# Loads through one ring, uneven groups and moved casts in an attention and feed-forward kernel

## The chip, the cores and the metric

The kernel runs on one core of a Trainium2 chip. A core has a matrix engine (PE, whose weight loads are shown as PEld), a vector engine (DVE), a scalar engine (ACT), a general-purpose engine (POOL) and a queue that issues transfers (SP); each works through its own instructions in order and waits on semaphores for the others. Sixteen DMA engines move data between HBM and the on-chip memory. The metric is device microseconds of one execution; lower is better.

## The reference

Inputs are q, k, v of shape (4, 8, 768, 64) in float32 and three weight matrices. Each head attends causally; the retrieval heads (0, 2 and 6) see all earlier keys, the five streaming heads only the first 4 keys and a window of 64. The result, as 3072 tokens of 512, goes through a gated feed-forward block.

```python
scores = scale * np.matmul(q, k.transpose(0, 1, 3, 2))
in_win = (rel >= 0) & (rel < int(window))          # window 64
stream_keep = causal & (is_sink | in_win)          # 4 sinks
mask = np.where(retrieval_head, causal, stream_keep)
a = softmax(np.where(mask, scores, -1e9))
x = np.matmul(a, v)      # to (B*S, H*D) = (3072, 512)
g = x @ w_gate           # (512, 1536)
out = (g * sigmoid(g) * (x @ w_val)) @ w_out       # (1536, 512)
```

## The kernel before, in words

**Units.** The 3072 tokens are 24 tiles of 128 (TT = 24; six per batch, i is the index in the batch). A tile goes through these steps; each is one item of a list:

- `load` (L74): three transfers of 256 KB on SP bring the tile's q, k and v in float32 into a ring of four landing buffers. Tiles 0 to 3 are loaded at the start; `cast(t)` issues the load of tile t + 4.
- `cast` (L186): q and k are cast to float16 on DVE (hq, L192, 512 elements each), v on POOL (vt, L196).
- `transposes` (L201): eight PE transposes of q and k, and a copy to qkT on DVE (L210); POOL then copies the sink keys and values (k2, v2: L213, L216 for i = 0) or the second half of the tile (L221, L223) into operands that hold "sinks and the tail of the previous tile" for streaming heads.
- `scores` (L256), one to four units a tile: up to eight 128x128 score blocks on PE into the one scores buffer in PSUM, exp on ACT (L272, L276) into e; masks are deferred to the next flush. In the first unit of a tile all blocks are masked at once on POOL (L281 for i = 0, L287 otherwise); in later units, one head's pair on POOL (L296) and the diagonal block of each retrieval head on DVE (L299), three a tile for i > 0.
- `values` (L306), for the odd and the even heads: matmuls of e with v, then reciprocal and a scaled copy on DVE (xb, L317, L318).
- `xtranspose` (L324): four transposes and a DVE copy to xt (L332), the feed-forward's input.

**The order of items.** For tile t the list interleaves its scores units with values of t-1 (even), transposes of t+1, values of t (odd) and xtranspose of t-1. cast(t+2) stands just before the transposes of t+1, so a cast is a whole tile ahead of its use.

**Groups.** The feed-forward takes four tiles at a time (GT = 4, six groups). The *lead* is all attention items through xtranspose(3), run alone, with a flush after each item; by the order above it also holds tile 4's scores and tile 5's transposes. Then for each group g and each of 12 blocks j: `gate` (four matmuls of 512 columns, tanh on ACT, L410), a *beat*, `val` (four matmuls, then sil L421 and h L424 on DVE), a beat, `outproj` of group g-1 (four matmuls, L436; every third one ends an output tile, which ACT copies, L441, and SP stores), a beat. Each beat flushes masks and runs a share of the attention items for the tiles of group g + 1. Three PSUM buffers serve gate and val, one the output, one the scores, one all transposes. After the last group its 48 output matmuls run alone.

**Weights.** They come as 18 pieces of 512 KB through their own ring of five landing buffers (`wload`, L143), and are cast to float16: gate pieces on DVE (L161), val and out pieces on POOL (L165, L158). `wstep` casts the next piece and loads up to five ahead; it is called with 4 after the lead and with 2 after each j of group 0:

```python
    lead = ends[GT - 1]
    for n in range(lead):
        attend(n + 1)
        flush()
    wstep(4)
```

**Constants.** POOL builds the identity, the masks (diag, band0, m1, and m0 by eight copies, L121) and fills k2 and v2 with zeros (L131, L132) before its first cast.

Of the kernel before, what the change touches and what calls it, by code (L numbers as in the profile page):

```python
# [7 lines left out]
FP = mybir.dt.float32  # L8
# [7 lines left out]
def kernel(  # L16
# [27 lines left out]
    GT = 4  # L44
    NG = TT // GT
# [9 lines left out]
    wstage = ctx.enter_context(tc.tile_pool(name="wstage", bufs=5))  # L55
    raw = ctx.enter_context(tc.tile_pool(name="raw", bufs=4))
# [15 lines left out]
    raws = {}  # L72

    def load(t):  # L74
        b, i = divmod(t, NT)
        sl = slice(i * 128, (i + 1) * 128)
        qk = raw.tile([128, 2, 8, 64], FP, name="rawqk", tag="rawqk")
        vr = raw.tile([128, 8, 64], FP, name="rawv", tag="rawv")
        nc.sync.dma_start(out=qk[:, 0], in_=q[b, :, sl, :].rearrange("h s d -> s h d"))
        nc.sync.dma_start(out=qk[:, 1], in_=k[b, :, sl, :].rearrange("h s d -> s h d"))  # L80
        nc.sync.dma_start(out=vr, in_=v[b, :, sl, :].rearrange("h s d -> s h d"))
        raws[t] = (qk, vr)

    for t in range(4):
        load(t)
# [34 lines left out]
    for n_, src in enumerate((band0, band0, band0, diag, band0, band0, diag, diag)):  # L120
        nc.gpsimd.tensor_copy(out=m0[:, n_, :], in_=src)  # L121
# [7 lines left out]
    for n in range(2):  # L129
        nc.gpsimd.memset(vt[n][:, :, :, 64:66], 1.0)  # L130
        nc.gpsimd.memset(k2[n], 0.0)  # L131
        nc.gpsimd.memset(v2[n], 0.0)  # L132


    wg_sb = const.tile([128, 4, DFF], FH, name="wg_sb")
    wv_sb = const.tile([128, 4, DFF], FH, name="wv_sb")
    wo_sb = const.tile([128, NJ, DM], FH, name="wo_sb")
    wgd = moe_w_gate.rearrange("(po p) n -> p po n", p=128)
    wvd = moe_w_val.rearrange("(po p) n -> p po n", p=128)
    wod = moe_w_out.rearrange("(po p) n -> p po n", p=128)  # L140
    staged = {}

    def wload(kind, c):  # L143
        st = wstage.tile([128, 1024], FP, name="wst", tag="wst")
        if kind == "o":
            nc.sync.dma_start(
                out=st.rearrange("p (a n) -> p a n", a=2), in_=wod[:, 2 * c:2 * c + 2, :])
        else:
            d = wgd if kind == "g" else wvd
            nc.sync.dma_start(  # L150
                out=st.rearrange("p (a n) -> p a n", a=4),
                in_=d[:, :, c * 256:(c + 1) * 256])
        staged[kind, c] = st

    def wcast(kind, c):
        st = staged.pop((kind, c))
        if kind == "o":
            nc.gpsimd.tensor_copy(  # L158
                out=wo_sb[:, 2 * c:2 * c + 2, :], in_=st.rearrange("p (a n) -> p a n", a=2))
        elif kind == "g":  # L160
            nc.vector.tensor_copy(  # L161
                out=wg_sb[:, :, c * 256:(c + 1) * 256],
                in_=st.rearrange("p (a n) -> p a n", a=4))
        else:
            nc.gpsimd.tensor_copy(  # L165
                out=wv_sb[:, :, c * 256:(c + 1) * 256],
                in_=st.rearrange("p (a n) -> p a n", a=4))

    worder = [(kd, c) for c in range(NJ // 2) for kd in "gv"] + [("o", c) for c in range(NJ // 2)]
    wnext = [0, 0]  # L170

    def wstep(n=1):

        for _ in range(n):
            if wnext[1] >= len(worder):
                return
            while wnext[0] < len(worder) and wnext[0] < wnext[1] + 5:
                wload(*worder[wnext[0]])
                wnext[0] += 1
            wcast(*worder[wnext[1]])  # L180
            wnext[1] += 1
# [4 lines left out]
    def cast(t):  # L186

        b, i = divmod(t, NT)
        qk, vr = raws.pop(t)
        hq = half.tile([128, 2, 2, 256], FH, name="hq", tag="hq")  # L190
        for n in range(2):
            nc.vector.tensor_copy(  # L192
                out=hq[:, n].rearrange("p r (k d) -> p r k d", d=64),
                in_=qk[:, n].rearrange("p (k r) d -> p r k d", r=2),
            )
        nc.gpsimd.tensor_copy(out=vt[b % 2][:, i, :, 0:64], in_=vr)  # L196
        halves[t] = hq
        if t + 4 < TT:
            load(t + 4)
# [56 lines left out]
    def scores(t, u, unit):  # L256
# [22 lines left out]
        def masks():  # L279
            if i == 0:  # L280
                nc.gpsimd.tensor_tensor(  # L281
# [3 lines left out]
            if u == 0:  # L285
                ev = e.rearrange("p s (h n) q -> p (s h) (n q)", n=2)
                nc.gpsimd.tensor_tensor(  # L287
# [4 lines left out]
            for s in range(2):  # L292
                for n, (h, m, total, _, _) in enumerate(unit[s]):
# [4 lines left out]
                    elif m == total - 1:  # L298
                        nc.vector.tensor_tensor(  # L299
# [24 lines left out]
    def xtranspose(t):  # L324
        g, n = divmod(t, GT)
        if g not in xts:
            xts[g] = xtp.tile([128, 4, GT * 128], FH, name="xt", tag="xt")
# [9 lines left out]
    def add(cost, f, *a):  # L337
        items.append((cost, f, a))

    def tile_items(t):  # L340
        ss = []
        if t < TT:
            units = plan_of(t)
            ss = [(0.3, scores, (t, u, None)) for u in range(len(units))]
        other = []
        if t > 0:
            other.append((0.4, values, (t - 1, 0)))
        if t + 1 < TT:
            other.append((0.5, transposes, (t + 1,)))
# [163 lines left out]
```

## Time and profile before

| | us |
|---|---|
| median of 3 runs (lowest to highest) | 317.99 (317.45 to 320.77) |
| the profiled execution | 320.0 |
| its span, first to last instruction | 318.3 |
| PE busy | 263.1 (83%) |
| DVE busy | 212.0 (67%) |
| ACT busy | 116.3 (37%) |
| POOL busy | 132.5 (42%) |

A row of a view in order of time gives start, length, engine, line, operation, output, inputs, count, and in brackets the idle time ahead of it and what ended it. A row of the groups gives busy time and the mean in ns, and then the idle time before the group's instructions. A row of the chain gives start, length and what was on the path that set the end. A PE row's length contains about 0.24 us of pipeline beyond the streaming of its columns, so a run of matmuls is priced by the distance of their starts.

### The profile page before, as it was taken

What the parts mean: (1) busy time and instruction counts of PE and PEld (TensorE: products, weight loads), DVE (VectorE), ACT (ScalarE), POOL (GpSimd) and SP (SyncE); (2) the same over time, 40 slices, a digit from 0 to 9 for tenths busy, and PEclk for the clock granted to TensorE, in tenths of its full rate; (3) what the DMA queues carried; (4) which work ended last, traced back from release to release, by engine and by line L of the source; (5) the groups of instructions that cost most, each with busy time, mean ns of one, the idle gap of its engine ahead of it and who ended that gap; (6) DMA issues with size and microseconds to landing.
All of it is one profiled execution on the core that took longest, in us unless ns stands there. A gap on an engine that the chain in (4) does not pass through costs nothing.

```text
span 318.3 us, 5386 instructions
## 1 busy us (share of the span) xinstructions
PE 263.1 (83%) x2096; PEld 133.0 (42%) x2096; DVE 212.0 (67%) x402; ACT 116.3 (37%) x177; POOL 132.5 (42%) x152
## 2 busy tenths in 40 slices
PE   0035761976886999998999999999899998999984
PEld 0024541433442454453545444544445444444431
DVE  4996583699997666786878757777776655555500
ACT  1023441350431445534353445245344453333211
POOL 8885761585991540643535416445143030000000
PEclk9999999997998999999999999999999999999999
DMA  8996548999844045505552534000000000000021
GB/s 184 217 209 148 134 100 216 381 298 348 244 103 99 13 121 134 129 6 132 132 123 62 132 85 103 33 33 35 33 2 33 35 33 16 20 33 35 38 94 66
DMA packets 86328, 34.94 MB, mean 110 GB/s; under 512 B 75552, under 2 KB 81696, under 8 KB 86304
## 3 DMA queue, kind: packets, MB, share of 16 engines
q1 hardware_dynamic: 86304, 34.61, 40.0%
q8 instruction: 16, 0.26, 0.3%
q14 instruction: 8, 0.07, 0.1%
HBM read 28.31 MB, written 6.29 MB: 109 GB/s over the span
## 4 chain that ended last, share of the span: by engine, by line
PE 67%; DVE 14%; DMA 6%; POOL 5%; ACT 4%; SPq 1%; issue 1%; DVEq 0%; ACTq 0%; POOLq 0%
PE o_ps L436 20%; PE gate L406 18%; PE val L417 17%; DVE hq L192 8%; PE sc L266 6%; ACT e L272 3%; PE av L314 3%; PE tr L207 2%; DMA wst<-in_moe_w_val_dram 2%; DMA wst<-in_moe_w_out_dram 2%; DMA wst<-in_moe_w_gate_dram 2%; DVE h L424 2%; PE xtr L331 1%; DVE qkT L210 1%; DVE e L299 1%
## 5 line engine op out<-in xcount | busy, mean ns | idle before, releaser
L406 PE MATMUL gate<-xt,wg_sb 128*128 128x512 f16 x288 | 75.5, 385 | 12.6 <-DVE wg_sb L161 7.0
L421 DVE SCALAR_TENSOR_TENSOR sil<-sig,gate 128x512 f32<-128x512 f32 x72 | 49.2, 684 | 45.7 <-ACT sig L410 45.6
L410 ACT ACTIVATE sig<-gate 128x512 f32<-128x512 f32 x72 | 43.0, 597 | 100.2 <-PE gate L406 100.2
L417 PE MATMUL val<-xt,wv_sb 128*128 128x512 f16 x288 | 76.5, 389 | 1.8 <-DVE sil L421 1.8
L436 PE MATMUL o_ps<-wo_sb,h 128*128 128x512 f16 x288 | 73.4, 382 | 2.8 <-ACT o_sb L441 2.8
L287 POOL TENSOR_TENSOR e<-e,m 128x1024 f16<-128x1024 f16 x20 | 42.6, 2132 | 66.3 <-ACT e L272 66.3
L272 ACT ACTIVATE e<-sc 128x1024 f16<-128x1024 f32 x48 | 49.1, 1022 | 53.3 <-PE sc L266 49.1
L424 DVE SCALAR_TENSOR_TENSOR h<-sil,val 128x512 f16<-128x512 f32 x72 | 49.5, 688 | 8.4 <-PE val L417 0.7
L192 DVE CAST hq<-rawqk 128x512 f16<-128x512 f32 x48 | 45.2, 981 | 4.4 <-DMA rawqk<-in_q_dram 4.0
L406 PEld LDWEIGHTS <-wg_sb 128*128 128x128 f16 x288 | 25.4, 99 | 37.6 <-issue 7.8
L417 PEld LDWEIGHTS <-wv_sb 128*128 128x128 f16 x288 | 25.8, 99 | 30.5 <-issue 3.3
L436 PEld LDWEIGHTS <-h 128*128 128x128 f16 x288 | 25.8, 98 | 30.1 <-issue 4.7
L266 PE MATMUL sc<-qkT 64*128 64x128 f16 x392 | 27.9, 236 | 4.8 <-ACT e L272 2.4
L314 PE MATMUL av<-vt,e 128*128 128x65 f16 x392 | 23.9, 201 | 8.5 <-POOL e L281 3.6
L314 PEld LDWEIGHTS <-e 128*128 128x128 f16 x472 | 21.7, 102 | 20.8 <-POOL e L281 3.8
L207 PE MATMUL tr<-ident,hq 128*128 128x128 f16 x192 | 17.4, 242 | 13.9 <-DVE hq L192 13.9
L266 PEld LDWEIGHTS <-qkT 64*128 64x128 f16 x392 | 15.7, 100 | 30.0 <-issue 26.7
L441 ACT COPY o_sb<-o_ps 128x512 f32<-128x512 f32 x24 | 14.1, 586 | 35.1 <-PE o_ps L436 35.1
L299 DVE TENSOR_TENSOR e<-e,diag 128x128 f16<-128x128 f16 x60 | 19.0, 346 | 9.6 <-ACT e L272 8.2
L207 PEld LDWEIGHTS <-hq 128*128 128x128 f16 x192 | 14.1, 108 | 19.5 <-DVE hq L192 14.3
L318 DVE TENSOR_TENSOR xb<-av,rc 128x256 f16<-128x256 f32 x48 | 20.4, 424 | 1.7
L296 POOL TENSOR_TENSOR e<-e,m 128x256 f16<-128x256 f16 x20 | 13.9, 697 | 10.5 <-ACT e L272 10.4
(39 smaller groups left out, 176.9 us busy)
## 6 DMA issues: line engine op xcount, KB each, us to landing
rawqk<-in_q_dram SPq DMA_DIRECT2D x24, 256.0 KB, 2.9
rawqk<-in_k_dram SPq DMA_DIRECT2D x24, 256.0 KB, 3.5
rawv<-in_v_dram SPq DMA_DIRECT2D x24, 256.0 KB, 3.9
out_dram<-o_sb SPq DMA_DIRECT2D x24, 256.0 KB, 2.0
wst<-in_moe_w_gate_dram SPq DMA_DIRECT2D x6, 512.0 KB, 5.7
wst<-in_moe_w_val_dram SPq DMA_DIRECT2D x6, 512.0 KB, 5.9
wst<-in_moe_w_out_dram SPq DMA_DIRECT2D x6, 512.0 KB, 5.6
```

What stands on the lines that cost most here:

```text
L192: nc.vector.tensor_copy(out=hq[:, n].rearrange("p r (k d) -> p r k d", d=64), in_=qk[:, n].rearrange("p (k r) d -> p r k d", r=2),)
L207: nc.tensor.transpose(tr[:, n, p, :], hq[:, n, p // 2, (p % 2) * 128:(p % 2 + 1) * 128], ident)
L266: nc.tensor.matmul(sc[:, s, n, :], kk, T[s * 64:s * 64 + 64, 0, p, i * 128:(i + 1) * 128])
L272: nc.scalar.activation(out=e[:, :, 0:na], in_=sc[:, :, 0:na], func=AF.Exp, scale=scale)
L287: nc.gpsimd.tensor_tensor(out=ev, in0=ev, in1=m1.rearrange("p n q -> p (n q)").unsqueeze(1).to_broadcast([128, 4, 256]), op=ALU.mult)
L314: nc.tensor.matmul(av[:, n, 0:65], ee, vv, start=(m == 0), stop=(m == len(bl) - 1))
L406: nc.tensor.matmul(ps, wg_sb[:, kk, j * 128:(j + 1) * 128], xt[:, kk, :], start=(kk == 0), stop=(kk == 3))
L410: nc.scalar.activation(out=sig, in_=ps, func=AF.Tanh, scale=0.5)
L417: nc.tensor.matmul(pv, wv_sb[:, kk, j * 128:(j + 1) * 128], xt[:, kk, :], start=(kk == 0), stop=(kk == 3))
L421: nc.vector.scalar_tensor_tensor(out=sil, in0=sig, scalar=1.0, op0=ALU.add, in1=ps, op1=ALU.mult)
L424: nc.vector.scalar_tensor_tensor(out=h, in0=sil, scalar=0.5, op0=ALU.mult, in1=pv, op1=ALU.mult)
L436: nc.tensor.matmul(o_ps, hs[g, j][:, tt * 128:(tt + 1) * 128], wo_sb[:, j, :], start=(j == 0), stop=(j == NJ - 1))
```

## The change

- **One ring.** Tile loads and weight pieces share one pool of seven landing buffers of 128 x 1536 float32 (786 KB). Weight pieces are now 1536 elements wide, four each of gate (g), val (v) and out (o). The order of loads is written out: tiles 0 to 3; g0 v0 g1 v1 g2 v2; tile 4; g3 v3; tile 5; o0 to o3; tile 6 and on. Seven loads are issued at the start, and one more after each cast (`freed`), into the buffer that the cast frees.
- **Weight casts.** g0, v0 are cast at j = 0 of group 0, g1, v1 at j = 3, and so on; the o pieces at j = 0 and 1 of group 1. g, o0 and o2 are cast on ACT, v, o1 and o3 on POOL.
- **Tile casts.** q and k are cast on ACT, except q of tiles 0 to 3, which stays on DVE. cast(t+1) now stands just before the transposes of t+1.
- **Masks.** The first unit's mask is on DVE for tiles 0 to 3 and on POOL after them; the diagonal blocks are on POOL.
- **Constants.** The eight copies to m0 and the zero fills are on DVE; only the parts of k2 and v2 that nothing else writes are filled (1024 and 2112 elements a partition, twice).
- **Groups** of 4, 2, 4, 4, 4, 4 and 2 tiles. In a group of two, gate and val matmuls, tanh, sil and h have 256 columns. `outproj` is spread evenly over the j of a group, from j = 2 on in group 1.
- **Order.** The lead ends with values and xtranspose of tile 3, with nothing of tile 4 in it; tile 4's cast and transposes are the first items of group 0. Group 0 then has 24 items (those of tiles 4 and 5, and the first parts of 6 and 7) in 24 beats.

The diff, cut to its core:

```diff
-    GT = 4
-    NG = TT // GT
+    SIZES = [4, 2, 4, 4, 4, 4, 2]
+    LEAD = SIZES[0]
...
-    wstage = ctx.enter_context(tc.tile_pool(name="wstage", bufs=5))
-    raw = ctx.enter_context(tc.tile_pool(name="raw", bufs=4))
+    raw = ctx.enter_context(tc.tile_pool(name="raw", bufs=7))
...
+    def load(what):
+        r = raw.tile([128, 1536], FP, name="raw", tag="raw")
+        landed[what] = r
...
+            for w, src in enumerate((q, k, v)):
+                nc.sync.dma_start(out=rv[:, w], in_=src[b, :, sl, :].rearrange("h s d -> s h d"))
...
+    def wcast(what):
...
+        if kind == "v" or (kind == "o" and n % 2):
+            nc.gpsimd.tensor_copy(out=dst, in_=src)
+        else:
+            nc.scalar.copy(out=dst, in_=src)
+
+    order = [("t", t) for t in range(LEAD)]
+    order += [(kd, n) for n in range(3) for kd in "gv"] + [("t", LEAD)]
+    order += [("g", 3), ("v", 3), ("t", LEAD + 1)] + [("o", n) for n in range(4)]
+    order += [("t", t) for t in range(LEAD + 2, TT)]
...
+    freed(7)
...
-        nc.gpsimd.tensor_copy(out=m0[:, n_, :], in_=src)
+        nc.vector.tensor_copy(out=m0[:, n_, :], in_=src)
...
-        nc.gpsimd.memset(k2[n], 0.0)
-        nc.gpsimd.memset(v2[n], 0.0)
+        nc.vector.memset(k2[n][:, :, :, 0:64], 0.0)
+        nc.vector.memset(v2[n][0:64], 0.0)
...
-            nc.vector.tensor_copy(
-                out=hq[:, n].rearrange("p r (k d) -> p r k d", d=64),
-                in_=qk[:, n].rearrange("p (k r) d -> p r k d", r=2),
-            )
-        nc.gpsimd.tensor_copy(out=vt[b % 2][:, i, :, 0:64], in_=vr)
+            if t < LEAD and n == 0:
+                nc.vector.tensor_copy(out=o_, in_=i_)
+            else:
+                nc.scalar.copy(out=o_, in_=i_)
+        nc.gpsimd.tensor_copy(out=vt[b % 2][:, i, :, 0:64], in_=r[:, 2])
         halves[t] = hq
-        if t + 4 < TT:
-            load(t + 4)
+        freed()
...
-                nc.gpsimd.tensor_tensor(
+                (nc.vector if t < LEAD else nc.gpsimd).tensor_tensor(
                     out=ev, in0=ev,
...
-                        nc.vector.tensor_tensor(
+                        nc.gpsimd.tensor_tensor(
                             out=e[:, s, n], in0=e[:, s, n], in1=diag, op=ALU.mult)
...
+        if t + 1 < TT and t + 1 != LEAD:
+            other += [(0.0, cast, t + 1), (0.5, transposes, t + 1)]
...
+        if t == LEAD:
+
+            add(0.4, values, t - 1, 0)
+            add(0.25, xtranspose, t - 1)
+            add(0.0, cast, t)
+            add(0.5, transposes, t)
+        weave(ss, other)
...
-    wstep(4)
     for g in range(NG):
         start = pos[0]
-        stop = ends[min(GT * (g + 2), TT) - 1]
-        beats = NJ * (3 if g else 2)
-        done = 0
+        stop = ends[FIRST[g + 2] - 1] if g + 2 <= NG else len(items)
+        n_out = SIZES[g - 1] * 3 if g else 0
+        beats = NJ * 2 + n_out
+        done = outs = 0
+        late = 2 if g == 1 else 0
...
         for j in range(NJ):
+            if g == 0 and j % 3 == 0:
+                for kd in "gv":
+                    wcast((kd, j // 3))
+                    freed()
+            if g == 1 and j < 2:
+                for n in (2 * j, 2 * j + 1):
+                    wcast(("o", n))
+                    freed()
             ps, sig = gate(g, j)
             beat()
             val(g, j, ps, sig)
             beat()
-            if g:
-                outproj(g - 1, j)
+            while outs * (NJ - late) < n_out * (j + 1 - late):
+                outproj(g - 1, outs)
+                outs += 1
                 beat()
-            else:
-                wstep(2)
-    for n in range(NJ):
+    for n in range(SIZES[NG - 1] * 3):
         outproj(NG - 1, n)
```

More of the change, by code (lines that the diff above doesn't have):

```diff
@@ L43 @@
     TT = B * NT
-    GT = 4
-    NG = TT // GT
+    SIZES = [4, 2, 4, 4, 4, 4, 2]
+    NG = len(SIZES)
+    FIRST = [sum(SIZES[:g]) for g in range(NG + 1)]
+    assert FIRST[NG] == TT
+    GROUP = {t: (g, t - FIRST[g]) for g in range(NG) for t in range(FIRST[g], FIRST[g + 1])}
+    LEAD = SIZES[0]
     scale = 1.0 / (D ** 0.5)
```

173 lines of the change are left out of this document (70 added, 103 removed).

## The prediction

> **What bounds the kernel now.** I read the stages first (busy time between chosen moments), then the chain that ended last, then the rows in order of time, then the groups. The stage boundaries are the first scores, the last copy of the lead into xt, the first gate matmul, the first gate of group 1, the first of group 5, and the tail.
>
> ```profile
> span 318.3 us, 5386 instructions
> ...
> 4.58:15.87 11.29, 1.21 (x8) 0.69 (x9) 10.26 (x3) 0.00 (x0) 10.24 (x17) 1.00 1.02 232
> ...
> 49.90:56.44 6.54, 0.00 (x1) 0.01 (x1) 1.10 (x3) 0.00 (x0) 0.00 (x0) 1.00 1.02 284
> 56.44:100.27 43.83, 34.58 (x292) 17.09 (x293) 39.18 (x70) 15.52 (x23) 31.88 (x31) 0.96 0.86 261
> 100.27:268.50 168.23, 164.85 (x1381) 82.01 (x1380) 118.16 (x252) 75.01 (x116) 63.02 (x63) 0.99 0.25 67
> 268.50:299.90 31.40, 30.88 (x147) 14.05 (x146) 15.79 (x25) 9.52 (x16) 0.00 (x0) 1.00 0.09 34
> 299.90:318.30 18.40, 11.87 (x53) 4.86 (x50) 1.19 (x2) 2.93 (x5) 0.00 (x0) 1.00 0.19 71
> ```
>
> Columns: stage, length, then PE, PEld, DVE, ACT, POOL busy, clock, DMA share, GB/s. From 100.27 on PE is busy 98% of the time: that part is bound by PE and pays only for less work. The first 100 us are not: PE is busy 1.2 of the 11.3 us before the first scores, idle from 49.90 to 56.44, and busy 34.6 of the 43.8 of group 0. The chain says why:
>
> ```profile
> 4.91 9.52 DVE hq L192
> 15.73 6.27 DVE hq L192 x4
> 26.15 1.70 DVE e L299 x3
> 50.61 5.06 DMA wst<-in_moe_w_gate_dram
> 55.69 0.70 DVE wg_sb L161
> 56.44 1.89 PE gate L406 x4
> 61.10 0.86 PE gate L406 x4
> ```
>
> One cast of 512 elements lasts 9.52 us, and four take 6.27, while POOL works without a gap; the weights are asked for only at 50.6, after the lead. The last two rows: four matmuls of 512 columns take 1.89 cold and 0.86 warm (0.216 each).
>
> **The start.** The m0 copies and the fills of k2 and v2 go from POOL to DVE, ahead of the first cast.
>
> ```profile
> 2.96 0.31 POOL L114 MEMSET m<- 128x256 f16 x1
> 4.72 0.20 POOL L119 MEMSET m<- 4x128 f16 x1
> 6.87 1.79 POOL L131 MEMSET k<- 128x2048 f16 x1
> 8.62 1.85 POOL L132 MEMSET v<- 128x2112 f16 x1
> 15.12 0.69 DVE L210 COPY qkT<-tr 128x1024 f16<-128x1024 f16 x1 [0.70 <-PE tr L207]
> 16.18 2.13 POOL L216 COPY v<-vt 4x2112 f16<-4x2112 f16 x1
> 16.41 1.03 PE L207 MATMUL tr<-ident,hq 128*128 128x128 f16 x8
> 27.77 0.75 DVE L192 CAST hq<-rawqk 128x512 f16<-128x512 f32 x2
> 49.76 0.21 DVE L299 TENSOR_TENSOR e<-e,diag 128x128 f16<-128x128 f16 x1
> ```
>
> band0 is ready at about 3.2. Eight copies at 0.21 (the nearest DVE row of 128 elements) end at 4.9, or at 7.0 if POOL's stream (to 5.3) holds them. No DVE fill is in the trace. At POOL's 0.875 ns an element, 2 x (1024 + 2112) elements are 5.5 us; at DVE's own 0.67 (qkT) 4.2, and as a fill reads nothing I let it go to 2.1; at the 1.34 of sil (684 ns for 512, quoted below), 8.4. I take 5.5: DVE is free at 10.4. Cast 0.4, transposes 1.03, qkT 0.7: first scores at 12.7 (9 to 17), against 15.87. A page of the Trainium skill speaks against the move: VectorE: DVE Perf Modes, section Zero memsets can be issued as uint32 (trn2), says that a memset takes one cycle per element whatever its type; that would be an estimated 6.5 us, and the sum 1.0 later; no run so far shows one.
>
> **The lead.**
>
> ```profile
> 15.87 0.61 PE L266 MATMUL sc<-qkT 64*128 64x128 f16 x8 [0.79 <-DVE qkT L210]
> ...
> 22.65 0.61 PE L266 MATMUL sc<-qkT 64*128 64x128 f16 x8 [1.24 <-DVE qkT L210]
> 23.30 1.02 ACT L272 ACTIVATE e<-sc 128x1024 f16<-128x1024 f32 x1 [5.76 <-PE sc L266]
> ...
> 29.69 0.29 PE L266 MATMUL sc<-qkT 64*128 64x128 f16 x2
> ```
>
> A tile now takes 6.8 to 7.0. After the change: scores 0.65, exp to 1.7, second scores, exp to 3.4 (one scores buffer), k cast on ACT to 4.0, transposes to 5.1, qkT to 5.8, the previous tile's xtranspose ahead of the next scores: 6.2. The first unit's mask on DVE (1024 elements: 0.7 at qkT's pace, 1.4 at sil's; I take 0.7, as the 128-element mask took 0.21) ends at 2.4 to 3.1, beside the second exp, where POOL's 2.13 stood before; then come one xb and the q cast (0.4), which must start before POOL masks the second unit from 3.45 on. In tile 0 POOL's sink copy (2.13) and vt cast hold the DVE mask and cast: 5.7 (4.6 to 6.1). Tile 3 has no next tile to prepare (before, the lead also held tile 4's scores and tile 5's transposes; these now count in group 0); its diagonal masks on POOL (below) end at 5.9, then values, xtranspose, xt: 8.5. First gate at 12.7 + 5.7 + 6.2 + 6.2 + 8.5 = **39.3**, instead of 56.44.
>
> Weights are no wait there: four tiles of 786 KB at 232 GB/s need 13.6 us, three pieces at 284 another 8.3, on SP behind the twelve tile transfers. So g0 and v0 have landed by 22. Their casts (1.45 on ACT, 1.6 on POOL, priced below) are hidden by tile 3's values, xtranspose and xt: ACT's last exp of the lead ends 3.6 before the gate, POOL's last mask 2.6; without that cover they would cost 1.6.
>
> **Group 0.** Prices:
>
> ```profile
> L421 DVE SCALAR_TENSOR_TENSOR sil<-sig,gate 128x512 f32<-128x512 f32 x72 | 49.2, 684 | 45.7 <-ACT sig L410 45.6
> L410 ACT ACTIVATE sig<-gate 128x512 f32<-128x512 f32 x72 | 43.0, 597 | 100.2 <-PE gate L406 100.2
> L272 ACT ACTIVATE e<-sc 128x1024 f16<-128x1024 f32 x48 | 49.1, 1022 | 53.3 <-PE sc L266 49.1 <-POOL v L223 2.4 <-POOL e L287 1.8
> L441 ACT COPY o_sb<-o_ps 128x512 f32<-128x512 f32 x24 | 14.1, 586 | 35.1 <-PE o_ps L436 35.1
> L287 POOL TENSOR_TENSOR e<-e,m 128x1024 f16<-128x1024 f16 x20 | 42.6, 2132 | 66.3 <-ACT e L272 66.3
> L296 POOL TENSOR_TENSOR e<-e,m 128x256 f16<-128x256 f16 x20 | 13.9, 697 | 10.5 <-ACT e L272 10.4
> L196 POOL CAST vt<-rawv 128x512 f16<-128x512 f32 x24 | 17.2, 716 | 0.0
> L165 POOL CAST wv_sb<-wst 128x1024 f16<-128x1024 f32 x6 | 7.0, 1172 | 13.3 <-DMA wst<-in_moe_w_val_dram 13.3
> rawqk<-in_k_dram SPq DMA_DIRECT2D x24, 256.0 KB, 3.5
> PE gate L406 <- DVE xt L332: 5.6, 5, 2.2
> ```
>
> ACT has 0.83 ns an element: a piece of 1536 costs 1.45, an hq cast 0.6. POOL: a v piece 1.6, a diagonal mask 0.46 (slope of the two mask rows). Work on PE: 96 matmuls x 0.216 = 20.7; tiles 4 and 5 at 2.74 each (168.23 less 576 x 0.216 is 43.8, over 16 tiles); the first parts of tiles 6 and 7, 1.5: 27.7 in all. There are 24 items for 24 beats, so each gate or val is followed by one item. Waits, walking through that order with these prices (a wait is the time that ACT's queue ends after PE arrives):
> - cold matmuls, 1.89 against 0.86, over some 3.4 us: 1.7;
> - transposes of tile 4 behind ACT's tanh and two casts: 1.0;
> - gate j=3 behind tanh, exp(4,1) and the 1.45 cast of g1: 2.6; j=6 likewise behind exp(5,1): 2.5; j=9, after an xtranspose instead: 0.6. If ACT ran ahead these were nothing;
> - tile 6: its load is issued when piece v2 is cast, at j=6, behind o3 on SP; cast(6) comes one beat later, and ACT waits for it with exp and tanh queued behind. 786 KB at 284 GB/s and the k row's 3.5 us: transposes of tile 6 are 2.5 late.
> Sum 38.6 (29 if all of ACT's waits are covered). **Group 1 starts at 77.9.** The v pieces and the masks on POOL cost nothing here: the gate before val hides a v cast that starts while PE waits for ACT; without that cover each would add up to 1.6. The tile loads and o pieces behind them on SP are needed only a group later, tile 6 excepted.
>
> **The rest.** Before: 168.23 + 31.40 + 18.40 = 218.0. Added: two tiles of attention not done by then (5.5) and two score units (0.7), one more group boundary (5.6 / 5 = 1.1), wo casts at j=0, 1 of group 1 (1.45 each on ACT before tanh: 1.5 of wait). Saved: two copies in the tail.
>
> ```profile
> 151.34 0.61 PE L207 MATMUL tr<-ident,hq 128*128 128x128 f16 x8
> ...
> L406 PEld LDWEIGHTS <-wg_sb 128*128 128x128 f16 x288 | 25.4, 99 | 37.6 <-issue 7.8
> ...
> 304.87 2.75 PE L436 MATMUL o_ps<-wo_sb,h 128*128 128x512 f16 x12 [0.67 <-ACT o_sb L441]
> ```
>
> That is 2 x 0.67 = 1.3. Matmuls of 256 columns in the two-tile groups are priced at half of 0.216: 128 columns come every (0.61 - 0.24) / 7 = 0.053; if a weight load of 0.1 showed behind each of 192, it would be 19 more. The hq casts, 1.2 a tile, now stand on ACT one or two beats ahead of their transposes, behind a tanh (0.6) or exp (1.02); a beat is about 1.2 of PE. I take 0.15 for each of 18 tiles, 2.7 (0 to 15). DVE loses 44 casts and 60 masks: of the 3.4 PE is idle in 168.23, I give back 1. So 218.0 + 5.5 + 0.7 + 1.1 + 1.5 - 1.3 + 2.7 - 1.0 = 227.2, and POOL's 60 diagonals (27 us) hide under its idle 105 of 168.
>
> **Sum.** 77.9 + 227.2 = 305.1 of span, 306.8 with the 1.7 by which the profiled execution's own 320.0 exceeds its span. The median, 317.99, is 2.0 below that execution: **304.8 us**.
>
> **The rivals.**
> 1. ACT's waits are covered. ACT's busy time is 15.5 of 43.8 in group 0 now; pieces have landed long before, so an in-order ACT may take them in a gap. Group 0 at 30 instead of 38.6, first scores at 9 to 11, steady waits nil: about 291. Against: each cast stands behind an exp that PE feeds just before.
> 2. The lock stays in the lead. If the DVE q cast misses the moment before POOL masks (0.67 and three times 0.46, then vt 0.7), it waits for that run's end, 2.6 a tile, in two tiles: 5.2, with the m0 copies held (2.1) and the fills at 8.4 (2.9): 10.2 in all, about 315. For it: 9.52 and 1.70 above. The Trainium skill, SBUF — State Buffer, Who interferes with whom, also has such locking between DVE and GpSimd; the rows of hq agree.
> 3. Slower: ACT becomes the bound of the steady part. tanh, exp and two casts in series are 2.8; where only one beat lies between cast and transposes, PE waits 1.6. From 0.15 + 13.2 / 18 = 0.9 a tile on, the gain is gone; at 1.6 it is 331. For it: casts and transposes now stand together. Against: ACT is busy 75.0 of 168.23, and some 22 us of casts leave it under 60%.
> 4. It doesn't do what it says: pieces arrive late since one blocked load holds all behind it on SP. Only tile 6 is asked for late by the order; if tiles 5 and 7 were as late, 5 to 7 us, 311, inside the range.
>
> **How the numbers follow.** Forecast with its own range 298 to 311: 0.54. Rival 1: 0.20; rival 2: 0.14; rival 4: 0.06; rival 3: 0.06. Faster by over 1% (about what a measurement can tell from no change) takes the forecast, rivals 1 and 4 and half of rival 2: 0.87; the other half and a little of rival 3 lie within 1%: 0.08; slower, the rest of rival 3: 0.05. The range reaches from rival 1 to just past rival 2 and leaves out what lies beyond them: 291 to 316.
>
> **What would show it.** Right: first scores near 13, first gate near 39, group 1 near 78, gate waiting for ACT's wg_sb at j=3 and 6, tile 6's ACT cast waiting for its DMA, and 227 from there with PE above 95%. Wrong: a DVE cast of several us in the lead, first gate after 45, or PE transposes waiting for ACT's hq in the later groups.

## The result and the profile after

The changed kernel takes 303.37 us (median of 4 runs, 301.71 to 305.26) against 318.64 for the kernel before on the same chip: a ratio of 0.952, 95% interval 0.944 to 0.959. The prediction was 304.8. The profiled execution took 303.0, its span 301.3; before they were 320.0 and 318.3, so the profile's difference is 17.0. One run each of fill_pool and fill_hq, and a few of the kernel before, fell in a slower state of the chip and are left out of the medians, ranges and ratios below.

The stages of the changed kernel, between its own marks (first scores, first gate, first gate of group 1, first of the last group, end), in the columns of the prediction's first fence:

```profile
9.58:34.65 25.07, 14.84 (x171) 11.15 (x172) 12.53 (x30) 11.45 (x15) 14.70 (x25) 1.00 0.91 274
34.65:77.87 43.22, 32.73 (x255) 15.15 (x255) 22.33 (x40) 24.31 (x34) 21.74 (x25) 0.96 0.75 212
77.87:269.67 191.80, 184.94 (x1593) 96.43 (x1593) 111.66 (x224) 102.71 (x170) 89.75 (x120) 1.00 0.31 79
269.67:301.30 31.63, 26.50 (x168) 16.33 (x167) 10.11 (x24) 7.83 (x18) 0.00 (x0) 0.99 0.16 59
```

The first scores come 6.3 earlier (15.87 before). From there to the first gate it is 25.07 instead of 40.57: 15.5 less. Of these, 6.5 are the wait for the first weights (49.90 to 56.44 before), 5.6 lie in the lead's last stretch (13.44 from 36.46; 7.79 now), which no longer holds tile 4's scores and tile 5's transposes, and 3.3 in the three tiles ahead of it. Group 0 is as long as it was (43.22; 43.83 before): it now holds that work of tile 4 and tile 5, but prepares two tiles instead of four, and PE is at work in only 32.73 of it. The rest is 5.4 longer (223.43; 218.03), as attention left out of group 0 is done there. So the whole gain lies before the first gate, and part of what was gained there is work that moved.

The chain of work that ended last, from its start to group 1:

```profile
3.04 1.10 DVE m L165 x8
4.19 0.48 DVE k L175
4.84 0.94 DVE v L176
...
38.65 3.73 DMA raw<-in_k_dram
44.43 1.37 ACT wg_sb L114
54.50 1.47 ACT wg_sb L114
56.45 5.72 DMA raw<-in_k_dram
67.00 1.47 ACT wg_sb L114
```

Neither the cast of 9.52 nor the transfer of g0 stands on it any more. In group 0 it runs through the casts of three gate pieces and through the k transfers of two tiles. PE's rows in order of time show what each of these costs (idle time ahead of a row in brackets):

```profile
34.65 1.87 PE L403 MATMUL gate<-xt,wg_sb 128*128 128x512 f16 x4 [0.52 <-DVE xt L328]
45.85 1.04 PE L403 MATMUL gate<-xt,wg_sb 128*128 128x512 f16 x4 [2.38 <-ACT wg_sb L114]
56.02 1.04 PE L403 MATMUL gate<-xt,wg_sb 128*128 128x512 f16 x4 [2.54 <-ACT wg_sb L114]
61.97 0.61 PE L203 MATMUL tr<-ident,hq 128*128 128x128 f16 x4 [2.75 <-ACT hq L192]
63.26 1.91 PE L414 MATMUL val<-xt,wv_sb 128*128 128x512 f16 x4
68.52 1.04 PE L403 MATMUL gate<-xt,wg_sb 128*128 128x512 f16 x4 [0.72 <-ACT wg_sb L114]
```

The three gates at 45.85, 56.02 and 68.52 wait for a cast; the transposes at 61.97 for tile 6's cast, which waits for its load; and the val at 63.26 is 1.91 long where a warm one is 1.04 (66.55): PE is cold again, at a granted clock of 0.53 from 63.20 to 65.20.

Last, the groups of instructions whose cost the prediction had to guess (busy, mean ns, then idle time):

```profile
L192 ACT CAST hq<-raw 128x512 f16<-128x512 f32 x44 | 25.4, 621 | 7.5 <-DMA raw<-in_q_dram 3.9 <-DMA raw<-in_k_dram 3.6
L114 ACT CAST wg_sb<-raw 128x1536 f16<-128x1536 f32 x4 | 5.9, 1468 | 0.0
L176 DVE MEMSET v<- 64x1056 uint32 x2 | 1.9, 938 | 0.3 <-issue 0.3
L175 DVE MEMSET k<- 128x512 uint32 x2 | 1.0, 485 | 0.1
```

The casts on ACT cost what was estimated (0.62 and 1.47, for 0.6 and 1.45); the two fills cost half.

### The profile page after: what moved, and what is told of

Same layout as the page of the kernel before. It is cut to its first block, busy times and chain, and to the rows that moved or that the text cites. A ratio compares the mean times of both kernels' runs of the same rounds, so it can differ in the third digit from the quotient of the medians.

```text
span 301.3 us, 5640 instructions
## 1 busy us (share of the span) xinstructions
PE 260.0 (86%) x2192; PEld 139.8 (46%) x2192; DVE 161.5 (54%) x332; ACT 148.2 (49%) x239; POOL 130.7 (43%) x190
## 4 chain that ended last, share of the span: by engine, by line
PE 75%; ACT 8%; DVE 8%; DMA 3%; issue 3%; POOL 1%; SPq 0%; ACTq 0%; DVEq 0%; POOLq 0%
PE gate L403 20%; PE o_ps L434 20%; PE val L414 18%; PE sc L262 7%; PE av L310 4%; PE tr L203 4%; DMA raw<-in_k_dram 3%; ACT e L268 3%; ACT hq L192 2%; PE xtr L327 2%; ACT wg_sb L114 1%; DVE qkT L206 1%; DVE h L421 1%; DVE xb L314 1%; ACT sig L407 1%
## 5 line engine op out<-in xcount | busy, mean ns | idle before, releaser
L418 DVE SCALAR_TENSOR_TENSOR sil<-sig,gate 128x512 f32<-128x512 f32 (+1 forms) x84 | 51.1, 609 | 71.1 <-ACT sig L407 71.0
L403 PE MATMUL gate<-xt,wg_sb 128*128 128x512 f16 (+1 forms) x336 | 77.1, 352 | 11.6 <-DVE xt L328 6.0
L407 ACT ACTIVATE sig<-gate 128x512 f32<-128x512 f32 (+1 forms) x84 | 45.0, 536 | 70.1 <-PE gate L403 69.5
L414 PE MATMUL val<-xt,wv_sb 128*128 128x512 f16 (+1 forms) x336 | 77.8, 355 | 1.2 <-DVE sil L418 1.2
L283 POOL TENSOR_TENSOR e<-e,m 128x1024 f16<-128x1024 f16 x17 | 36.1, 2123 | 51.8 <-ACT e L268 51.8
L421 DVE SCALAR_TENSOR_TENSOR h<-sil,val 128x512 f16<-128x512 f32 (+1 forms) x84 | 51.3, 611 | 9.1 <-PE val L414 0.5
L414 PEld LDWEIGHTS <-wv_sb 128*128 128x128 f16 x336 | 30.3, 99 | 25.6 <-issue 3.0
L295 POOL TENSOR_TENSOR e<-e,diag 128x128 f16<-128x128 f16 x60 | 24.8, 426 | 24.2 <-ACT e L272 14.1
L192 ACT CAST hq<-raw 128x512 f16<-128x512 f32 x44 | 25.4, 621 | 7.5 <-DMA raw<-in_q_dram 3.9
L206 DVE COPY qkT<-tr 128x1024 f16<-128x1024 f16 x24 | 16.6, 690 | 23.2 <-PE tr L203 20.3
L310 PEld LDWEIGHTS <-e 128*128 128x128 f16 x472 | 22.0, 102 | 10.3 <-DVE xb L314 1.1
```

The costliest lines, as they stand in the source:

```text
L192: nc.scalar.copy(out=o_, in_=i_)
L283: (nc.vector if t < LEAD else nc.gpsimd).tensor_tensor(out=ev, in0=ev, in1=m1.rearrange("p n q -> p (n q)").unsqueeze(1).to_broadcast([128 ...
L310: nc.tensor.matmul(av[:, n, 0:65], ee, vv, start=(m == 0), stop=(m == len(bl) - 1))
L403: nc.tensor.matmul(ps, wg_sb[:, kk, j * 128:(j + 1) * 128], xt[:, kk, 0:w], start=(kk == 0), stop=(kk == 3))
L407: nc.scalar.activation(out=sig, in_=ps, func=AF.Tanh, scale=0.5)
L414: nc.tensor.matmul(pv, wv_sb[:, kk, j * 128:(j + 1) * 128], xt[:, kk, 0:w], start=(kk == 0), stop=(kk == 3))
```

## The experiments

Eleven kernels, each the changed kernel with one or two parts undone or one or two more things done. Each ratio is to runs of the kernel before on its chip; "group 1" is the first gate of group 1 in the profiled execution.

| kernel | first scores | first gate | group 1 | median (range), us | ratio, 95% interval |
|---|---|---|---|---|---|
| changed kernel | 9.58 | 34.65 | 77.87 | 303.37 (301.71 to 305.26) | 0.952 (0.944 to 0.959) |
| fill_pool | 6.74 | 36.26 | 78.66 | 305.46 (303.85 to 306.87) | 0.960 (0.952 to 0.968) |
| mask_pool | 9.60 | 35.14 | 79.82 | 304.83 (304.2 to 306.09) | 0.959 (0.952 to 0.965) |
| hq_dve | 9.60 | 34.55 | 77.44 | 306.87 (304.79 to 307.46) | 0.963 (0.957 to 0.970) |
| fill_hq | 15.90 | 40.86 | 83.14 | 312.43 (308.43 to 312.54) | 0.972 (0.964 to 0.980) |
| late_weights | 9.60 | 34.01 | 73.93 | 300.69 (299.31 to 301.5) | 0.945 (0.939 to 0.950) |
| held | 9.59 | 41.70 | 87.83 | 311.26 (310.45 to 312.92) | 0.974 (0.968 to 0.980) |
| tiles_first | 9.59 | 34.66 | 73.65 | 299.04 (298.65 to 301.68) | 0.940 (0.935 to 0.945) |
| cast_early | 9.58 | 34.65 | 70.50 | 296.52 (295.63 to 297.23) | 0.931 (0.928 to 0.934) |
| wg_dve | 9.59 | 35.53 | 85.29 | 311.35 (310.12 to 312.92) | 0.977 (0.973 to 0.982) |
| uniform | 9.58 | 34.66 | 85.25 | 304.84 (303.85 to 305.89) | 0.957 (0.953 to 0.960) |
| both | 9.58 | 34.63 | 68.13 | 293.54 (292.77 to 294.51) | 0.920 (0.916 to 0.923) |

### fill_pool: constants back on POOL

```diff
-        nc.vector.tensor_copy(out=m0[:, n_, :], in_=src)
+        nc.gpsimd.tensor_copy(out=m0[:, n_, :], in_=src)
...
-        nc.vector.memset(k2[n][:, :, :, 0:64], 0.0)
-        nc.vector.memset(v2[n][0:64], 0.0)
+        nc.gpsimd.memset(k2[n], 0.0)
+        nc.gpsimd.memset(v2[n], 0.0)
```

> The changed kernel with the eight m0 copies and the whole fills of k2 and v2 back on POOL; all else as changed. My theory: the lock between POOL's long stream and two-port work on DVE held the start, and k's cast is now on ACT, so the first scores come no later (7.5 to 10 instead of 9.58), but POOL is busy until about 14 and only then casts v and copies the sinks, so tile 1's scores come at 17 to 19 instead of 14.88, the first gate at 37 to 39 instead of 34.65, and the time is 2.5 to 4 us over the changed kernel's 303.4. Rival: the whole 6.3 us by which the first scores moved came from these fills; then the first scores are back at about 15.9 and the time is 6 us longer. Second rival: it is hidden, within 1 us.

Measured: the first scores come 2.8 earlier, the first gate 1.6 later, group 1 0.8 later; the median is 2.1 longer, but the two intervals overlap, and the profiled spans differ by 0.8 (302.1; 301.3). DVE's rows in order of time:

```profile
3.78 0.48 DVE L190 CAST hq<-raw 128x512 f16<-128x512 f32 x1 [3.78 <-DMA raw<-in_q_dram]
...
9.13 5.29 DVE L190 CAST hq<-raw 128x512 f16<-128x512 f32 x1
```

Tile 0's q cast slips in before POOL's fills and its k is on ACT, so nothing holds it; tile 1's q cast falls into the fills and takes 5.29 instead of 0.83. The direction at the gate was that of my theory, the size (1.6) below its 2.4 to 4.4. The first rival, first scores back at 15.9, is refuted; the second, that the time hides it within 1 us, is not.

### fill_hq: that, and all q and k casts on DVE

```diff
-            if t < LEAD and n == 0:
+            if True:
                 nc.vector.tensor_copy(out=o_, in_=i_)
```

(and the diff of fill_pool)

> The changed kernel with two parts undone together: the m0 copies and the (full) fills of k2 and v2 are on POOL again, and every q and k cast is on DVE. My theory: either part alone keeps the first casts clear of POOL's stream of fills (fills on DVE, or k's cast on ACT), which is why undoing one of them cost 1 to 2 us in the lead or nothing; with both undone a DVE cast of 8 to 10 us is back in tile 0, first scores at 15 to 16 as in the kernel before, first gate at 40 to 42, the rest as with all casts on DVE (228): time 310 to 314. Rival: the two parts are independent and their losses add: first scores at 7 to 10, first gate at 36 to 37, time 308 to 309.

Measured: 15.90, 40.86 and 312.43, as my theory had it. DVE's rows of fill_hq, in order of time:

```profile
3.77 0.51 DVE L190 CAST hq<-raw 128x512 f16<-128x512 f32 x1 [3.77 <-DMA raw<-in_q_dram]
5.01 9.44 DVE L190 CAST hq<-raw 128x512 f16<-128x512 f32 x1 [0.73 <-DMA raw<-in_k_dram]
```

The cast of 9.52 is back, as one of 9.44. It is the second cast, of k, that meets the fills. So the two parts protect the same thing: the first scores come at 15.9 only when both are undone.

### hq_dve: all q and k casts on DVE

The edit is the diff of fill_hq without that of fill_pool.

> The changed kernel with all casts of q and k on DVE, as before. My theory: in the lead they are locked out by POOL, so the first gate comes 2 to 5 us later; after group 1 begins PE is the bound and nothing changes (223 from there, within 2); group 0 gains at most 1 from a shorter ACT queue. Time 1 to 5 us longer. Rival: ACT was overloaded by the casts, and taking them away shortens the part from group 1 on by 3 us or more.

Measured: the lead is not later (34.55), against my 2 to 5; what follows group 1 takes 228.4 instead of 223.4, against my two at most. The wait row of PE from its group 1 to its last group, and the stage:

```profile
PE tr L203 <- DVE hq L190: 3.3, 8, 0.9
...
77.44:274.12 196.68, 187.16 (x1592) 97.06 (x1592) 129.09 (x256) 87.27 (x138) 93.00 (x121) 0.99 0.30 77
```

The stage is 4.9 longer than that of the changed kernel (191.80), with 3.3 in 8 waits for a DVE cast where the changed kernel has 1.0 in two. Another 2.2 are PE's own time, in part at a lower clock in this execution (0.95 from 77.44 to 112, for 1.00), so they can't be put down to the casts. My theory was wrong in both places: the fear of a queue on ACT was misplaced, and by the waits DVE, with its own chain of sil, h and copies, is the worse place for these casts. The two medians' intervals still touch (0.957 to 0.970; 0.944 to 0.959).

### mask_pool: the lead's first-unit masks on POOL

```diff
-                (nc.vector if t < LEAD else nc.gpsimd).tensor_tensor(
+                nc.gpsimd.tensor_tensor(
```

> The changed kernel with the first unit's masks of tiles 0 to 3 back on POOL. My theory: the mask itself is not on the path, but POOL then runs without a gap from the first exp to its diagonal masks, and DVE's q cast (two-port) waits for it as the casts did before: about 2.5 us more in tiles 1 and 2 each and 1 in tile 0, first gate at 39 to 41 instead of 34.65, time 4 to 6 us longer. Rival: the mask has slack and PE's order hides it; first gate within 1 us of 34.65.

Measured: first gate 35.14, 0.5 later; the time is not distinguishable from the changed kernel's. The rival was right. DVE's and POOL's rows of mask_pool:

```profile
9.46 0.42 DVE L190 CAST hq<-raw 128x512 f16<-128x512 f32 x1
16.13 0.42 DVE L190 CAST hq<-raw 128x512 f16<-128x512 f32 x1
```

```profile
11.83 2.11 POOL L277 TENSOR_TENSOR e<-e,m 128x1024 f16<-128x1024 f16 x1
16.15 2.37 POOL L283 TENSOR_TENSOR e<-e,m 128x1024 f16<-128x1024 f16 x1 [0.62 <-ACT e L268]
```

With no mask ahead of it on DVE, the next tile's q cast runs before POOL's long run begins. The mask of 2.1 on POOL makes the values wait instead, for about the same.

### late_weights: weights asked for late, as I meant it

```diff
-    order += [(kd, n) for n in range(3) for kd in "gv"] + [("t", LEAD)]
-    order += [("g", 3), ("v", 3), ("t", LEAD + 1)] + [("o", n) for n in range(4)]
-    order += [("t", t) for t in range(LEAD + 2, TT)]
+    order += [("t", 4), ("g", 0), ("v", 0), ("t", 5), ("g", 1), ("v", 1), ("g", 2)]
+    order += [("v", 2), ("g", 3), ("v", 3), ("t", 6), ("t", 7)] + [("o", n) for n in range(4)]
+    order += [("t", t) for t in range(LEAD + 4, TT)]
+    hold = [True]
...
-        for _ in range(n):
+        for _ in range(0 if hold[0] and at[0] >= LEAD else n):
...
-    freed(7)
+    freed(LEAD)
...
+    hold[0] = False
+    freed(7)
     for g in range(NG):
```

> The changed kernel with the loads after the first four tiles held back until the lead is over, and then asked for in the order tile 4, g0, v0, tile 5, g1, v1, g2, v2, g3, v3, tiles 6 and 7, the o pieces. My theory: the first gate has to wait for tile 4 and g0, and its val for v0: 6 to 9 us of PE idle as in the kernel before, and later pieces arrive just in time, so the time is 6 to 10 us longer. Rival: the landing is hidden by the rest of group 0, whose ACT waits are there anyway: within 2 us.

Measured: 2.7 faster in the median (the intervals overlap), not slower, with group 1 3.9 earlier, at 73.93. The edit didn't hold the loads back, as SP's rows show:

```profile
12.28 1.01 SPq L94 DMA_DIRECT2D raw<-in_q_dram  x1
...
15.53 0.85 SPq L99 DMA_DIRECT2D raw<-in_moe_w_gate_dram  x1
```

The program issues these loads after the lead, but nothing else stands on SP, which runs through its own instructions as soon as a buffer is free. What the edit changed was only the order, with tiles 4 and 5 ahead. So this run says nothing of lateness; held does. It also changes how the kernel before is to be read: there the weights were asked for at 50.6 not because their code stands after the lead, but because they stood on SP behind the load of tile 10, which was issued only at 48.02, when tile 6's cast on DVE had freed its buffer.

### held: loads truly late

```diff
+    order += [("g", 0), ("v", 0), ("t", 4), ("g", 1), ("v", 1), ("t", 5), ("g", 2), ("v", 2)]
+    order += [("g", 3), ("v", 3), ("t", 6), ("t", 7)] + [("o", n) for n in range(4)]
...
+    mark = const.tile([1, 128], FH, name="mark")
+    nc.sync.dma_start(out=mark, in_=xts[0][0:1, 0, 384:512])
     hold[0] = False
     freed(7)
```

(on top of late_weights, in place of its order)

> What late_weights was meant to test and didn't: every load after tile 3 is now truly held until the lead is over. A small transfer out of xt (tile 3's part, the last copy of the lead) stands on SP ahead of them, so SP can't run past it; the order behind it is g0, v0, tile 4, g1, v1, tile 5, g2, v2 and so on, and it adds that one transfer of 256 bytes. Asked for at about 34, a piece of 786 KB at 284 GB/s takes 2.8 and some 2 until its end is seen, and its cast 1.47: first gate at 40 to 41 instead of 34.0 to 34.7 (in the kernel before the same wait was 6.5). v0 lands 2.8 after g0 and its cast on POOL takes 1.5, so the first val waits too; tile 4's cast comes another 2.8 later. My theory: loading early in one ring is worth these waits together: group 1 at 83 to 86 instead of 73.9 to 77.9, time 309 to 313. Rival: only the first wait shows, since ACT's casts and the masks delay group 0 anyway: group 1 at 82 or earlier, time 308 or less.

Measured: first gate 41.70, group 1 at 87.83, 311.26: my theory, with both stages a little past its ends. The chain of held:

```profile
34.28 0.62 SPq L449
...
35.56 6.55 DMA raw<-in_moe_w_val_dram
42.17 1.47 POOL wv_sb L112
...
44.09 8.33 DMA raw<-in_k_dram
```

The first gate waits 7.91 for g0's cast, and then the chain runs through two transfers, v0's and tile 5's. Against late_weights, whose order is nearly the same, early loading is worth 7.7 at the first gate, 13.9 at group 1 and 10.6 in the median. Part of the 6.2 between the two gates is clock: PE's own time in group 0 is 36.07 at a granted clock of 0.85 here, 33.35 at 0.90 in late_weights. No run keeps two rings and asks for the weights early, so what the shared ring itself is worth is open.

### tiles_first: the order of the ring

```diff
-    order += [(kd, n) for n in range(3) for kd in "gv"] + [("t", LEAD)]
-    order += [("g", 3), ("v", 3), ("t", LEAD + 1)] + [("o", n) for n in range(4)]
-    order += [("t", t) for t in range(LEAD + 2, TT)]
+    order += [(kd, n) for n in range(3) for kd in "gv"] + [("t", 4), ("t", 5)]
+    order += [("g", 3), ("v", 3), ("t", 6), ("t", 7), ("o", 0), ("t", 8)]
+    order += [("o", 1), ("o", 2), ("o", 3)] + [("t", t) for t in range(9, TT)]
```

> The changed kernel with another order of loads behind v2: tiles 4 and 5, g3, v3, tiles 6 and 7, o0, tile 8, o1 to o3. My theory: of group 0's 43.2 us, 2.75 and 0.29 are PE waiting for tile 6's ACT cast, whose load stood behind the o pieces, about 1.0 is PE cold after that wait, and 0.75 is tile 5's load; asked for earlier these vanish, group 1 starts at 73 to 74 instead of 77.87, and the time is 4 us shorter than the changed kernel's (299 to 300). Rival: ACT's queue is the real bound of group 0 and takes the time back in the gate waits; group 1 starts after 76.

Measured: 299.04 and 73.65, as expected. The wait of 2.75 for tile 6's cast is gone, and the gate at j=3 waits 1.49 instead of 2.38; PE's cold row moves to the gate at j=6:

```profile
44.90 1.04 PE L403 MATMUL gate<-xt,wg_sb 128*128 128x512 f16 x4 [1.49 <-ACT wg_sb L114]
55.07 1.89 PE L403 MATMUL gate<-xt,wg_sb 128*128 128x512 f16 x4 [2.54 <-ACT wg_sb L114]
```

### cast_early: pieces cast two blocks earlier

```diff
-            if g == 0 and j % 3 == 0:
+            if g == 0 and (j == 0 or j % 3 == 1 and j < 10):
                 for kd in "gv":
-                    wcast((kd, j // 3))
+                    wcast((kd, (j + 2) // 3))
```

> The changed kernel with the weight pieces cast two blocks ahead of their use (g1, v1 at j = 1, g2, v2 at 4, g3, v3 at 7), order of loads as changed. My theory: the waits of gate for ACT's casts at j = 3, 6, 9 (2.4, 2.5, 0.7) come from where the cast stands in ACT's queue and vanish, and tile 6's load, which follows v2's cast, is asked for two blocks sooner, so its 3.0 vanishes too; group 1 starts at 69 to 72 instead of 77.87, time 6 to 8 us under the changed kernel's. Rival: ACT has no slack in group 0 (24.3 us busy of 43.2, the rest waits on PE), so the cast delays tanh instead and PE waits there; gain under 3.

Measured: 296.52 and 70.50, as expected. No gate waits for a cast any more. Tile 6's wait did not vanish, though: its transposes still wait 1.13 and 0.54 (2.75 and 0.29 in the changed kernel), and the chain of cast_early still holds the two transfers:

```profile
38.66 3.89 DMA raw<-in_k_dram
...
48.48 7.41 DMA raw<-in_k_dram
```

### wg_dve: gate pieces cast on DVE

```diff
-        if kind == "v" or (kind == "o" and n % 2):
+        if kind == "g":
+            nc.vector.tensor_copy(out=dst, in_=src)
+        elif kind == "v" or (kind == "o" and n % 2):
```

> The changed kernel with the gate pieces cast on DVE instead of ACT, at the same places. My theory: DVE's queue ends earlier than ACT's at these places (it has no exp before the cast), a cast takes 1.0, so the waits at j = 3, 6, 9 fall from 5.6 to 2 in all and group 1 starts 2 to 4 sooner. Rival: DVE's cast is a two-port operation and is locked out by POOL's masks and v casts; then the waits stay or grow.

Measured: 311.35, 8 slower, with group 1 at 85.29. The rival was right. DVE's rows, two of POOL's and PE's waits in group 0 of wg_dve:

```profile
34.52 0.95 DVE L112 CAST wg_sb<-raw 128x1536 f16<-128x1536 f32 x1
46.51 1.85 DVE L112 CAST wg_sb<-raw 128x1536 f16<-128x1536 f32 x1
59.37 2.02 DVE L112 CAST wg_sb<-raw 128x1536 f16<-128x1536 f32 x1
```

```profile
46.08 1.46 POOL L114 CAST wv_sb<-raw 128x1536 f16<-128x1536 f32 x1
...
59.11 1.47 POOL L114 CAST wv_sb<-raw 128x1536 f16<-128x1536 f32 x1
```

```profile
PE gate L405 <- DVE wg_sb L112: 10.3, 4, 3.5
```

Alone (POOL has nothing from 34.40 to 40.77), a DVE cast of 1536 takes 0.95 (1.47 on ACT). At j = 3 and 6 the cast of the v piece starts on POOL just before it, and the DVE cast ends 0.8 after that one has ended, in twice the time. It also stands behind DVE's sil, h and copies. The gates wait 10.3: 1.4 at the first gate, where the changed kernel has no such wait, and 8.9 at j = 3, 6 and 9 instead of 5.6. After each of these three waits PE is cold (1.89).

### uniform: six groups of four, in the order of tiles_first

```diff
-    SIZES = [4, 2, 4, 4, 4, 4, 2]
+    SIZES = [4, 4, 4, 4, 4, 4]
```

> Six groups of four tiles, all else as changed, with the order of loads of tiles_first, which group 0 needs since it now holds four tiles' attention. My theory: the sizes are nearly neutral against tiles_first: 1.3 more in the tail, one boundary (1.1) less, half-width matmuls cost just half, and group 0's ACT waits are filled with 5.5 us of attention, so within 2 us of tiles_first. Rival: the small groups are worth something by themselves (fewer waits at both ends): uniform is 4 us or more slower. Second rival: group 0 with two tiles is starved; uniform is faster by 3 or more.

Measured: 304.84, 5.8 slower than tiles_first; the first rival was right. Group 0, tiles_first's and then uniform's:

```profile
34.66:73.65 38.99, 32.30 (x254) 15.04 (x254) 22.34 (x40) 23.99 (x34) 21.64 (x25) 0.96 0.86 237
```

```profile
34.66:85.25 50.59, 38.68 (x342) 19.78 (x341) 26.43 (x52) 30.50 (x44) 31.37 (x40) 0.93 0.78 208
```

With four tiles to prepare, PE has 6.4 more to do in group 0 but needs 11.6 more: ACT and POOL are each asked for about 31 of 50.6, and the chain of uniform runs over POOL:

```profile
68.08 2.13 POOL e L283
70.21 0.63 POOL e L292
...
73.64 1.47 POOL wv_sb L112
...
75.16 1.89 PE val L414 x4
```

What is left is 6.6 shorter than in tiles_first (216.85 against 223.45). The small second group thus keeps attention work out of group 0, where it doesn't fit under the weight casts. The run undoes the small last group too: outproj's matmuls in the tail wait 2.8 for ACT's copies instead of 1.3, so 1.5 of the difference belongs to that group.

### both: tiles_first and cast_early together

The edit is those two diffs.

> The two changes that helped, together: the order of loads of tiles_first (tiles 4 and 5 ahead of the pieces g3, v3 and the out pieces) and the weight pieces cast one or two blocks earlier, of cast_early. My theory: the waits they remove are different ones (tile loads that land late; gates that wait for a piece's cast), so the gains add up: first gate at 34.7 as before, group 1 at 66 to 68 (cast_early 70.5, tiles_first 73.7, the changed kernel 77.9), and 292 to 294 as the time. Rival: ACT's queue is the bound of group 0 once the casts stand earlier, and a load that lands sooner only moves the wait to ACT: group 1 at 70 or later, time 296 or more.

Measured: 293.54, group 1 at 68.13, just past the 66 to 68: the gains add up, nearly (4.2 and 7.4 apart, 9.7 together at group 1). Its group 0:

```profile
34.63:68.13 33.50, 31.37 (x255) 15.39 (x255) 22.25 (x40) 23.48 (x34) 21.60 (x25) 1.00 1.01 279
```

The same work with hardly a wait takes 33.50, PE busy in 31.37 of it. This version beats both kernels, at 0.920 of the kernel before.

## Why the prediction was right, point by point

**The start: the fills were mis-sized.** "I take 5.5" for the fills; they take 2.85 (twice 0.485 and 0.938), 3.2 with the gaps between them. The rows say why: they run as uint32, 512 and 1056 words, half the elements that I counted. The slope is (938 - 485) / (1056 - 512) = 0.83 ns a word. The section of the Trainium skill that I quoted (VectorE: DVE Perf Modes, Zero memsets can be issued as uint32 (trn2)) is about just this form; I used its cost for each element and not its halved count, by which the estimate would have been 3.3. The rows, at 2.85, are a little below that. The m0 copies took 1.1, not 1.7: their rows overlap, so a run of eight costs less than eight times the 0.22 of one. The cast, transposes and qkT behind them add 2.1 to the 10.4, which is 12.5; the 12.7 of the sum holds 0.2 that it doesn't name. First scores at 9.58 instead of 12.7; fill_hq shows that the mechanism was right (9.44 back) and fill_pool adds what I had not seen, that k's cast on ACT alone is enough for tile 0.

**The lead.** "5.7 + 6.2 + 6.2 + 8.5" measured 5.30, 5.86, 6.12 and 7.79 from first scores to first scores (9.58, 14.88, 20.74, 26.86) and to the first gate, 25.07 in all instead of 26.6. With the start that makes 34.65 for my 39.3. Rival 2 did not come: no DVE cast in the lead passed 0.9. Nor is it the mask on DVE that spares the lead, as I expected of mask_pool: that run refutes it. What made tiles 0 to 2 shorter than before (17.28; 20.59) is not shown: fill_hq, with every q and k cast on DVE, takes 24.96 from first scores to first gate, as little as the changed kernel.

**Group 0: right in kind, 4.6 short.** The waits that I walked through are there in their places: 2.38 for 2.6, 2.54 for 2.5, 0.72 for 0.6, and 3.04 for 2.5 at tile 6 (2.75, and 0.29 ahead of its second half, in PE's waits). Tile 4's transposes did not wait (1.0 predicted). What failed most is the other half of the sum, "27.7 in all" of work and 1.7 cold: PE's own time is 32.73, 3.3 more. Of this 1.4 is cold time that the waits bring with them (both, without them, is busy 31.37), as at 63.26, where a val is 0.87 longer; the other 2.0 is work that I priced by steady slopes. (My 1.89 and 0.86 were not like for like: a warm row of four is 1.03 long, and 0.86 is the distance of starts.) The last 1.3 is idle time, 10.49 for my 9.2: the sum had no term for the 1.36 that the next group's first gate waits for xt. Rival 1, "29 if all of ACT's waits are covered", did not happen by itself, since an in-order ACT reaches each cast only behind the exp and tanh ahead of it (44.32 after an exp from 43.41, in ACT's rows). cast_early brings it about by moving the casts up: 35.85, and both 33.50. No run came to 29; PE's own time alone is 31.37.

**Two errors cancelled.** 39.3 was 4.65 too late and 38.6 was 4.62 too short, so group 1 starts at 77.87 for my 77.9. That agreement is chance. So, in part, is that of the total: the span was forecast 3.8 too long (305.1; 301.3), the median only 1.4 (304.8; 303.37), because I took off 2.0 by which the profiled execution before lay above its median, and the one after lies 0.4 below its own.

**The rest: 3.8 too long.** "2.7 (0 to 15)" for hq casts that come late was 1.0, in PE's waits of the changed kernel from 77.9 to 269 (total, times, longest):

```profile
PE gate L403 <- DVE xt L328: 4.9, 5, 1.4
...
PE tr L203 <- ACT hq L192: 1.0, 2, 0.6
```

So rival 3 falls, and by its waits hq_dve has ACT as the better place. The larger part is in the base: the 218.0 of the kernel before holds a loss of its own. Its groups 1 and 2 in the stages view:

```profile
100.27:145.16 44.89, 43.34 (x365) 21.55 (x365) 31.53 (x65) 19.73 (x30) 17.49 (x17) 0.96 0.32 81
145.16:186.60 41.44, 41.01 (x343) 20.38 (x343) 30.92 (x68) 19.37 (x31) 17.09 (x18) 1.00 0.45 111
```

Group 1 takes 3.4 more than group 2, at a clock of 0.96, for nearly the same work (83 and 82 score blocks by the code). I took it over as if it were work. The trace of the kernel before says what most of it was. PE's granted clock was 0.64 from 100.27 to 104.00 and 0.91 from there to 108.00, then 1.00, which loses about 1.7 us; and the idle time at the group's end is 1.1 longer (1.55; 0.43). The clock fell right after the wait of 2.15 ahead of 100.27. In the changed kernel's profile the same stretch is at 1.00; in other runs it is not (0.95 behind group 1's start in late_weights and wg_dve), so this loss comes and goes between executions. With 1.7 (2.7 less 1.0) and 3.4 taken off, 227.2 becomes 222.1, and 223.4 was measured. The half-width groups cost just half: gate and val follow each other by 0.43 (269.67 to 270.10), four matmuls of 256 columns. PE is busy 94.6% of the 223.4, not above 95%; before, it was 98% up to 299.90 only, and 95% with the tail.

**The things it was said to do.** Rival 4, late pieces, did not occur: only tile loads were late (tiles 5 and 6, of which I had foreseen one). held prices what was avoided: about 8 at the first gate and 14 by group 1. Taken together, the 21.8 by which the first gate moved have two sources that the runs confirm: loads early enough (held, 7.7) and no DVE cast inside a POOL run (fill_hq, 6.2). Another 5.6 is work of tiles 4 and 5 that moved behind the gate, which the rows show and no run undoes, and for the rest no cause was shown. uniform adds that the small groups, the second above all, keep another 5.8 from being given back.

## What to carry to other kernels

In an in-order queue, a cast that is issued where its result is needed waits behind everything that the consumer itself feeds; issue it two blocks earlier (7 us here, 5.6 of it the gates' waits) and order the loads by when they are needed, not by kind (4 us). A load issued later in the program isn't later on a queue that has nothing else to wait for, and one behind a load that waits for a buffer is late wherever its code stands: read the queue's own rows before saying that a transfer is late. And when stages are priced from the profile of before, look at whether two equal stages took equal time, since a loss in the base is otherwise carried over as work.

## What was not expected of the hardware

- DVE's zero fills of float16 buffers run as uint32, 0.83 ns a word, half the count that the code shows.
- PE goes cold quickly: after idle time of 2.5 to 2.8 us a run of four 512-column matmuls took 1.89 to 1.91 instead of 1.04 (55.07 in tiles_first, 63.26 in the changed kernel), yet the gate at 56.02, after 2.54, took 1.04. In tiles_first the granted clock fell from 1.00 to 0.50 while PE was idle, about 1.9 us into the wait; in the changed kernel it stayed at 1.00 through the wait of the same length. The length of the wait alone doesn't decide it, and what does was not tried. The clock view doesn't show every cold stretch: at 34.65 it has 1.00, and the gate took 1.87.
- A DVE cast of 512 elements took 9.44 and 9.52 beside gapless POOL fills in two different kernels, and one of 1536 took 0.95 or 2.02 by what POOL did. The Trainium skill, SBUF — State Buffer, Who interferes with whom, has DVE and GpSimd lock each other out, for the whole of an instruction. The cast of 2.02 agrees; the one of 9.44 shows more, since no single POOL instruction beside it is longer than 1.85: it got in only at the end of POOL's run of fills.
